# Four of sixteen row groups turned by DMA, and a deeper fold of the mirrored groups, in a fused FFT and state-space kernel

## The chip, the cores and the metric

The kernel runs on one core of a Trainium2 chip, in one launch. The metric is the device time of that launch in microseconds. A run of the kernel before has 306.61 us as its median of three (306.09 to 307.59).

## The reference

The input x has 2048 tokens of 1024 features, in bf16. Two results are mixed by a gate that is one number for each token:

```
g = sigmoid((x * gate_w).sum(-1))
a = irfft2(rfft2(x) * W)                       # over tokens and features
b = S5 recurrence: h_t = Lam_bar * h_(t-1) + B_bar x_t ;  b = 2 Re(C h) + x * Dskip
out = g * a + (1 - g) * b
```

The states h are 1024 complex numbers. Everything is kept in bf16 with float32 sums on TensorE.

## The kernel before, in words

The kernel is written as generators, one for each kind of step (turn a row group, fold it, multiply it, move a result out of PSUM, store it). The string ORDER holds one letter for each step, and the kernel is issued in the order of that string; PIECES gives the order in which the small vector steps of the recurrence (letter "v") are taken, and SLOTS says which of four PSUM buffers each product gets. No scheduler comes behind this: each engine works through its own part of the list in order, and semaphores make it wait for the others. So one instruction that waits holds up everything that its engine was given after it.

**The Fourier side.** The tokens are taken as 16 row groups j of 128 tokens. `load_x` reads x, two row groups to a DMA. `turn` (L901) turns a row group on TensorE with eight 128x128 transposes, and `turn_out` (L906) copies the result from PSUM into xQ on ScalarE. `fold` (L920 to L926) forms sums and differences of feature halves on VectorE: L920 the odd part, L922 the sums, L925 and L926 sums and differences of those. The first four row groups are folded one at a time, the others in pairs. For the pairs named in MIRROR (row groups 8 to 15) the odd part is folded once more: `mirror` (L942) reverses it on TensorE, and `fold_odd` (L948, L949) adds and subtracts. `fd` (L419 to L426) multiplies a row group by the tables in G_sb: the odd half with 4 matmuls of 512 columns (L423), or 4 of 256 where it is mirrored (L419), and the even half with 4 matmuls of 256 columns (L426). `fd_out` (L433) and `s1_out` (L458) move the results out of PSUM, some on VectorE (FD_DVE, S1_DVE) and the rest on ScalarE. `s1` (L446) is the next DFT stage; later come `s2`, `times_w` (L601), `is1` and `is2`, with turns through DRAM between them, and `spectral` (L809 to L828), which unfolds the inverse transform on VectorE.

**The recurrence side.** `unit_mm` (L387) multiplies xQ by the B tables, in 8 chunks c of 256 tokens; it needs all sixteen row groups in xQ and the B tables, which come as transposing DMAs (`load_B`, L248). `unit_out` (L397) copies to h on ScalarE. `recur` does the recurrence of one chunk on VectorE: products with tables (L336, L339), sums (L342, L345), the carry (L348), two scans (L352), the carry out (L357, L360), products again, and the two last operations L363 and L367, after which h of the chunk may be read. `early_mm`, `own_mm` (L697, L711) multiply h by C for one token tile of 128 at a time. Chunk 7 is token tiles 14 and 15, whose products are the last ones (L711); `last_out` (L883) scales and adds them on VectorE, and `last_store` writes them out. The last tile is cut at its end into two pieces of 256 columns:

```python
    rest[-1:] = [(15, K, H), (15, K + H, H)]
```

The angles of the tables are made on ScalarE for the indices in ANG_ACT (L268) and on VectorE for the rest (L270); the casts of the tables are on ScalarE for those in CAST_ACT and on GpSimd for the rest (L276, L283).

Of the kernel before, what the change touches and what calls it, by code (L numbers as in the profile page):

```python
# [21 lines left out]
D = 1024  # L22
# [7 lines left out]
NHA, NHB = 2, 1  # L30
NSEP = 2
DIAG = (10, 11, 12)

WARM = 7
FD_DVE = (0, 1, 3, 7, 8)
CAST_ACT = (6, 7)
ANG_ACT = (0, 4, 5, 6)
CARRY_POOL = ()
S1_DVE = (1, 2, 3)
CLOSES = (0, 1, 2, 3, 10, 4, 5, 11, 12, 6, 7, 8, 9)  # L40
PIECES = (
# [6 lines left out]
)  # L48
SLOTS = (
    "0123013201301230123012301230120312301320123023102310213021302130230123121320320123021321201323023120",  # L50
    "3201231031231203201230130121231023012301201201303201320132013231032103012031",
)
MIRROR = (6, 7, 8, 9)
ORDER = (
    "xTxUfTVVfxVGTVVUUfVaaTfGVffaFFfxTxff2UaEtfTfaxfFUTxk2SbUEffEUAxFx1TTSTfEUFTUtAFf2US1bTbEfffUbbbEASUA",
    "STfATU~FuTfUEtFUTfUFS~hbEtaEtFwuffFrtAttt1ttttStSb1bbgbbHErrf~AttffEfAFhb1uSttbErttSShetHtftrtfvttAv",
    "tbvktAAtvttHr1b1vvFverFheEtt~ttKHEhh1ttvSSttvtu11vccSHtvtHAtFhhtvKrwccc1tvvccAttAEHtHFEKKwvvtvhvvvvv",
    "vtc1cccttvc11SA1cvvvvwSvhhvvvvA1vKKsHecccHHenLssvvsssvvhMNMJWssnsnvHsssvNvWLMsvvvsvjvnsMJWYWMYMs3Mv4",
    "h4NJ53Nv54Hvvvvv45h6J7H7hvvjym35m44nv56n7H7YM56nv88v3NN78W8WJM8vvyn4+vvj754Nh5YvM+HmN+h34vvyvvh5vMMJ",
    "JWm8M6hH473m7Hh5+M+48ndmHHdvJY86v4+nv5n7NWMJ7N3J4yv8MYjn4vv56N7vvmN+vvX87h5v8v5vy3Jhv8m4+455H6mh7H78",  # L60
    "8nJYH6m77v+hNymn+HY+vvvyvnNNmh8+vvv8JqiivJqqvnimI+hihvvvviYqiJyYdIhNiivvqImiqHHInqiY+ImJHIiHyvvvIqmI",
    "vviIIII%+niiIvvvyINmN+hvvminidIvvnvIlvlhpXHlzXNplvvNJ+mzZHPzPzhhHlHZZZZZpYJJ+o+QmQRRyRJ+RRZDRzZplRZO",
    "ZRZDPzvZQoYQPBvvvvZDOolZvoOzlZOZRZZQDRoovzBlQRRvoBZZZZRZZRvBvQCDDDOOzDlpopvBBYDPYzZvZZDZQ9oZZQ0oPRDR",
    "9RyRRRCyD9oo9C909oY900QD000",
)

EVEN = ((0, 0), (2, 1), (2, 0), (0, 1))
# [6 lines left out]
def _host_consts():  # L74
# [7 lines left out]
        G[cls, :, 1] = -np.sin(ang)  # L82
    G[0, :, 1, 0] = (-1.0) ** np.arange(K)
    Ge = np.stack([G[0, :H, :, e::2] for e in range(2)])
    Go = np.stack([G[1, :, :, e::2] for e in range(2)], axis=1)

    n = np.arange(H)[None, :] + 0.5
    Gi = np.zeros((4, 2, P, H))
    for u in range(4):
# [35 lines left out]
    b16 = lambda z: np.ascontiguousarray(np.asarray(z, dtype=np.float32).astype(ml_dtypes.bfloat16))  # L125
    return dict(
        G=b16(np.concatenate([Go.reshape(4, P, 4 * K // 4).transpose(1, 0, 2).reshape(P, 4 * K),
                              Ge.reshape(2, 2, P, H).transpose(2, 0, 1, 3).reshape(P, 4 * H)], axis=1)),
        Gi=b16(Gi),
        T2=b16(np.concatenate([Ts, Tc, -Ts], axis=2)),  # L130
        K3=b16(np.stack([Kc, Ks], axis=1)),
# [7 lines left out]
def kernel(  # L139
# [58 lines left out]
    def psum(shape, name, dtype=FP32):  # L198
        return ps.tile(shape, dtype, name=name, tag=next(slots, "ps"), bufs=1 if SLOTS else 4)
# [20 lines left out]

    xn = [CT[i // 4][:, 2 * (i % 4):2 * (i % 4) + 2, :] for i in range(8)]
    x_v = x.rearrange("(p j) d -> p j d", j=16)
    fft = {}
    fft["G"] = pre.tile([P, 4 * K + 4 * H], BF16, name="G_sb")
# [184 lines left out]
    def fd():  # L409
        T2_sb, G_sb = fft["T2"], fft["G"]  # L410
        Go = G_sb[:, 0:4 * K].rearrange("p (d n) -> p d n", d=4)
        Ge = G_sb[:, 4 * K:4 * K + 4 * H].rearrange("p (e d n) -> p e d n", e=2, d=2)
        for j in range(16):
            psd = psf[j] = psum([P, 2, K], "ps_fd")
            if mirrored(j):
                odd = psd[:, 1, :].rearrange("p (e r m) -> p r e m", e=2, r=2)
                for r in range(2):
                    for d2 in range(2):
                        nc.tensor.matmul(odd[:, r], lhsT=preTs[j][:, 4 + 2 * r + d2, :], rhs=Go[:, d2].rearrange("p (e r m) -> p r e m", e=2, r=2)[:, r],  # L419
                                         start=(d2 == 0), stop=(d2 == 1))  # L420
# [3 lines left out]
            for e in range(2):  # L424
                for d2 in range(2):
                    nc.tensor.matmul(psd[:, 0, H * e:H * (e + 1)], lhsT=preTs[j][:, 2 * e + d2, :], rhs=Ge[:, e, d2, :],  # L426
                                     start=(d2 == 0), stop=(d2 == 1))
            yield

    def fd_out():  # L430
# [373 lines left out]
    def spectral(tbs):  # L804
        for tb in tbs[1::2]:
            part, eo = part_of(tb)
            ev = halves_of[:, 0:2, 0:K].rearrange("p i (c n) -> p i c n", c=2)
            xy = part[:, :, 0:K].rearrange("p i (s c n) -> p i s c n", s=2, c=2)
            nc.vector.tensor_add(out=ev[:, :, :, 0:P], in0=xy[:, :, 0], in1=xy[:, :, 1])  # L809
            yield  # L810
            nc.vector.tensor_sub(out=ev[:, :, :, H - 1:P - 1:-1], in0=xy[:, :, 0], in1=xy[:, :, 1])
# [12 lines left out]
            part = part.rearrange("p i (s c n) -> p i s c n", s=2, c=2)  # L824
            ga = part.rearrange("p i s c n -> p i s (c n)")
            nc.vector.tensor_add(out=ga[:, :, 0], in0=eo[:, :, 0], in1=eo[:, :, 1])
            yield
            nc.vector.tensor_sub(out=ga[:, :, 1], in0=eo[:, :, 0], in1=eo[:, :, 1])  # L828
            for t in (tb - 1, tb):
                gas[t] = ga[:, t % 2]  # L830
            yield

    def add_late():
# [61 lines left out]
    pts = {}  # L895

    def turn():
        for j in range(16):
            pt = pts[j] = psum([P, 8, P], "pt", BF16)
            for i in range(8):  # L900
                nc.tensor.transpose(out=pt[:, i, :], in_=xn[j // 2][:, j % 2, P * i:P * (i + 1)], identity=ident)  # L901
            yield

    def turn_out():
        for j in range(16):
            nc.scalar.copy(out=x_gjq[:, :, :, :, j, :].rearrange("p c d g q -> p d c g q"),  # L906
                           in_=pts.pop(j).rearrange("p d (c q g) -> p d c g q", c=NCH, g=2))
            yield

    def fold():  # L910
        for j, n in [(j, 1) for j in range(4)] + [(j, 2) for j in range(4, 16, 2)]:
# [10 lines left out]
            nc.vector.tensor_add(out=apart(pairs["s"][:, at]), in0=lo, in1=hi)  # L922
            yield
            s_lo, s_hi = pairs["s"][:, at, 0:2], pairs["s"][:, at, 2:4]
            nc.vector.tensor_add(out=pairs["t"][:, at, 0:2], in0=s_lo, in1=s_hi)  # L925
            nc.vector.tensor_sub(out=pairs["t"][:, at, 2:4], in0=s_lo, in1=s_hi)  # L926
            yield

    mirrors = {}
# [79 lines left out]
    def load_Wcols():  # L1009
        nc.gpsimd.memset(unit_w[:, 0:1], 1.0)  # L1010
        nc.gpsimd.memset(unit_w[:, 1:2], 0.0)
        nc.gpsimd.tensor_copy(out=Wp.rearrange("p r b c -> p (r b c)"), in_=xn[7][:, 0, 0:64])
        nc.gpsimd.tensor_copy(out=Wf, in_=xn[7][:, 0, 0:2])
# [166 lines left out]
```

## Time and profile before

| | before |
|---|---|
| median of 3 runs | 306.61 us |
| the profiled execution | 306.76 us, span 305.0 us |
| TensorE busy | 297.3 us (97%) |
| VectorE busy | 289.8 us (95%) |
| ScalarE busy | 186.6 us (61%) |
| GpSimd busy | 73.8 us (24%) |
| DMA engines, mean of the span | 194 GB/s |

The span is the time from the first to the last instruction in the profile; 1.76 us of the execution lie outside it. PE is TensorE, DVE is VectorE, ACT is ScalarE, POOL is GpSimd, SP is the engine that issues most DMAs. In a timeline the columns are start, duration, engine, line, operation, the tiles (out<-in), shapes and count; what stands in brackets is the idle time just before, and what ended it.

### The profile page before, as it was taken

To read this page: it belongs to the slowest core of one execution; us is meant where nothing else is said; L and a number is where in the kernel's file an instruction comes from. 1 tells how busy PE (TensorE), PEld (TensorE's weight loads), DVE (VectorE), ACT (ScalarE), POOL (GpSimd) and SP (SyncE) were. 2 spreads that over 40 slices of the span, in tenths; PEclk is the share of its full clock that TensorE was granted. 3 is DMA by queue.
4 is the path that set the end of the run, shared out by engine and by line. 5 is a ranking of instruction groups with operands and counts; after the bars stand their busy time and mean duration, and the time that the engine had idled before them with its cause. 6 is when DMAs were issued, how large, how long until landed. Compare 5 with 4: busy or idle time off the path is not lost.

```text
span 305.0 us, 6407 instructions
## 1 busy us (share of the span) xinstructions
PE 297.3 (97%) x2576; PEld 199.2 (65%) x2598; DVE 289.8 (95%) x335; ACT 186.6 (61%) x251; POOL 73.8 (24%) x100
## 2 busy tenths in 40 slices
PE   6999999999999999999999999999999999999995
PEld 3666768878864684377744766679775896555544
DVE  0999999999999999999999998999999999999995
ACT  3999998787721477556665975365875866342400
POOL 1110344467554002002110212011112134344130
PEclk9799999999999999999999999999999999999999
DMA  6989998499999997989959877885898368996975
GB/s 214 376 291 181 219 181 221 74 205 119 273 189 267 250 269 145 260 247 232 221 103 198 191 176 201 271 206 145 195 237 178 98 79 168 153 127 147 186 114 169
DMA packets 70141, 59.29 MB, mean 194 GB/s; under 512 B 40632, under 2 KB 57536, under 8 KB 70112
## 3 DMA queue, kind: packets, MB, share of 16 engines
q1 hardware_dynamic: 63120, 50.18, 63.4%
q0 software_dynamic: 6912, 8.69, 23.9%
q8 instruction: 20, 0.33, 0.5%
q14 instruction: 9, 0.07, 0.1%
q10 hardware_dynamic: 80, 0.01, 0.0%
HBM read 28.45 MB, written 23.08 MB: 169 GB/s over the span
## 4 chain that ended last, share of the span: by engine, by line
PE 91%; DVE 5%; DMA 2%; issue 1%; ACTq 0%; DVEq 0%
PE psu L387 37%; PE ps_y L697 29%; PE ps_q L711 7%; PE ps_is L613 3%; PE ps_is L645 2%; PE ps_id L794 2%; PE ps_s L446 2%; PE ps_fd L426 2%; DMA vec<-in_gate_w_dram 2%; PE ps_s L578 1%; PE ps_fd L419 1%; PE ps_id L790 1%; DVE X L433 1%; PE ps_fd L423 1%; DVE CT L458 1%
## 5 line engine op out<-in xcount | busy, mean ns | idle before, releaser
L387 PE MATMUL psu<-xQ,BT 128*128 128x256 bf16 x1024 | 116.3, 273 | 0.0
L387 PEld LDWEIGHTS <-BT 128*128 128x128 bf16 x1024 | 99.0, 98 | 16.9 <-issue 5.0
L697 PE MATMUL ps_y<-CT,h 128*128 128x512 bf16 x399 | 92.4, 379 | 0.8
L352 DVE TENSOR_TENSOR_SCAN h<-rz,h 128x2048 bf16<-128x2048 f32 (+1 forms) x20 | 71.1, 3577 | 0.0
L697 PEld LDWEIGHTS <-h 128*128 128x128 bf16 x416 | 39.8, 98 | 46.3 <-issue 2.5
L769 POOL DMA_DIRECT2D y_scratch<-su x20 | 17.5, 904 | 136.7 <-ACT su L763 91.0
L397 ACT CAST h<-psu 128x1024 bf16<-128x1024 f32 x32 | 32.3, 1012 | 17.3 <-PE psu L387 14.8
L339 DVE TENSOR_TENSOR h<-h,tab 128x4096 bf16<-128x4096 bf16 (+1 forms) x20 | 37.3, 1865 | 0.5
L728 ACT ACTIVATE ye<-ps_y,omg 128x512 f32<-128x512 f32 x26 | 17.5, 689 | 28.0 <-PE ps_y L703 13.4
L336 DVE TENSOR_TENSOR xQ<-h,tab 128x4096 bf16<-128x4096 bf16 x12 | 27.4, 2287 | 1.4 <-ACT h L397 1.2
L587 ACT CAST X<-ps_s 128x1024 bf16<-128x1024 f32 x16 | 16.1, 1008 | 15.0 <-PE ps_s L578 15.0
L655 ACT CAST ZT<-ps_is 128x1024 bf16<-128x1024 f32 x16 | 15.8, 1014 | 9.6 <-PE ps_is L645 9.6
L711 PE MATMUL ps_q<-CT,h 128*128 128x512 bf16 (+1 forms) x110 | 21.1, 348 | 0.1
L621 ACT CAST C<-ps_is 128x1024 bf16<-128x1024 f32 x16 | 16.1, 1014 | 8.0 <-PE ps_is L613 6.6
L835 POOL DMA_DIRECT2D BT<-y_scratch x10 | 14.4, 1592 | 22.0 <-DVE BT L828 12.1
L801 ACT ACTIVATE BT<-ps_id,gB 128x1024 bf16<-128x1024 f32 x14 | 15.3, 1115 | 6.6 <-PE ps_id L794 5.1
L711 PEld LDWEIGHTS <-h 128*128 128x128 bf16 x112 | 11.0, 98 | 9.4
L906 ACT COPY xQ<-pt 128x1024 bf16<-128x1024 bf16 x16 | 15.7, 1016 | 1.7 <-PE pt L901 1.7
L763 ACT ACTIVATE su<-xs,omg 128x512 f32<-128x512 bf16 x20 | 14.3, 723 | 0.7 <-DVE xs L753 0.6
L433 ACT CAST X<-ps_fd 128x1024 bf16<-128x1024 f32 x11 | 11.2, 1020 | 0.1
L920 DVE TENSOR_TENSOR preT<-xQ 128x1024 bf16<-128x1024 bf16 (+1 forms) x10 | 5.8, 579 | 5.2 <-ACT xQ L906 5.0
L901 PEld LDWEIGHTS <-CT 128*128 128x128 bf16 x128 | 8.7, 104 | 2.3 <-issue 1.5
(188 smaller groups left out, 395.3 us busy)
## 6 DMA issues: line engine op xcount, KB each, us to landing
y_scratch<-ye SPq DMA_DIRECT2D x20, 256.0 KB, 3.4
y_scratch<-su POOLq DMA_DIRECT2D x20, 256.0 KB, 4.5
Bb<-turn_scratch SPq DMA_DIRECT2D x16, 256.0 KB, 5.3
turn_scratch<-C SPq DMA_DIRECT2D x16, 256.0 KB, 3.8
raw<-turn_scratch SPq DMA_DIRECT2D x8, 512.0 KB, 3.7
CT<-in_A_x_dram SPq DMA_DIRECT2D x7, 512.0 KB, 7.4
xs<-in_A_x_dram SPq DMA_DIRECT2D x13, 256.0 KB, 3.0
out_dram<-BT SPq DMA_DIRECT2D x11, 256.0 KB, 3.6
```

Source lines behind the costliest of these rows:

```text
L336: nc.vector.tensor_mul(out=tmps["s"], in0=u[:, ::-1], in1=bc(i))
L339: nc.vector.tensor_mul(out=u, in0=u, in1=bc(i))
L352: nc.vector.tensor_tensor_scan(out=seg, data0=rz[:, js.start + j:js.start + j + m].rearrange("p j t -> p (j t)"), data1=seg, initial=0.0, ...
L387: nc.tensor.matmul(psu[:, j, :], lhsT=BT[4 * q + j][:, ri, d8, :], rhs=xQ[:, c, d8, :], start=(d8 == 0), stop=(d8 == 7))
L397: nc.scalar.copy(out=hs[c][:, ri, 4 * q:4 * q + 4].rearrange("p b (q j) -> p b q j", j=32), in_=psus.pop((c, q, ri)).rearrange("p b (j q) ...
L587: nc.scalar.copy(out=X2, in_=ps2s[g][b])
L621: nc.scalar.copy(out=C1.rearrange("p h (u i) -> p h u i", u=4), in_=pscs[g][t].rearrange("p h (i u) -> p h u i", u=4))
L655: nc.scalar.copy(out=ZT[:, 4 * kp:4 * kp + 4, :, 4 * G:4 * G + 4].rearrange("p (c r) n g -> p c r n g", c=2), in_=pszs.pop((G, kp)).rearra ...
L697: nc.tensor.matmul(psy, lhsT=hs[c][:, ri, jb, P * tq:P * (tq + 1)], rhs=CT[ri][:, jb, 512 * dh:512 * (dh + 1)], start=(i == 0), stop=(i == ...
L711: nc.tensor.matmul(psq, lhsT=hs[c][:, ri, jb, P * tq:P * (tq + 1)], rhs=CT[ri][:, jb, at:at + n], start=(i == 0), stop=(i == 15))
L728: nc.scalar.activation(out=ye, in_=psys[tb][:, K * hf:K * (hf + 1)], func=ACT.Copy, scale=omg[:, tb:tb + 1])
L769: nc.gpsimd.dma_start(out=y_dram[tb, hf], in_=xgs[tb, hf], accum_op=ALU.add)
```

## The change

- **Row groups 12 to 15 (NTURN = 12).** They are no longer loaded in two plain DMAs and turned on TensorE. Two transposing DMAs bring 64 rows of 4096 elements each straight into the place in SBUF where the plain rows lay, already turned, and `turn_out` copies them from there, with ScalarE as before, instead of from PSUM.
- **The even half of the mirrored row groups.** The lower quarter is folded once more on VectorE (one add in place, then an add and a subtract of half the size), and its product takes two matmuls of 128 columns where it took two of 256. A new table Gf of 256 columns comes with G_sb. The even product is now issued ahead of the odd one.
- **Tables.** The even table (with Gf) is loaded ahead of the odd one.
- **The last tile** is cut into 384 and 128 columns, not 256 and 256.
- **Who does what.** FD_DVE, S1_DVE, CAST_ACT and ANG_ACT name other indices: as many casts from PSUM on VectorE as before (5 and 3), one angle fewer there, and one table cast fewer on ScalarE and one more on GpSimd.
- **Order.** ORDER, PIECES and SLOTS are new throughout.

```diff
+NTURN = 12
-FD_DVE = (0, 1, 3, 7, 8)
-CAST_ACT = (6, 7)
-ANG_ACT = (0, 4, 5, 6)
+FD_DVE = (1, 2, 3, 5, 9)
+CAST_ACT = (5,)
+ANG_ACT = (2, 4, 5, 6, 7)
-S1_DVE = (1, 2, 3)
+S1_DVE = (1, 3, 4)
...
+    Gf = np.concatenate([G[0, :P, :, 2 * f::4].reshape(P, P) for f in range(2)], axis=1)
...
+    x_sg = x.rearrange("(s g j) d -> g s (j d)", g=2, j=16)
+    xt = CT[1][:, 4:8].rearrange("p a k -> p (a k)").rearrange("p (j d g s) -> p j d g s", j=4, d=8, g=2)
...
     def load_x():
         for i in range(8):
+            if i >= NTURN // 2:
+                g = i - NTURN // 2
+                nc.sync.dma_start_transpose(out=xt[:, :, :, g].rearrange("p j d s -> p (j d) s"), in_=x_sg[g][:, NTURN * D:])
+                yield
+                continue
...
-        for a, b in ((0, 4 * K), (4 * K, 4 * K + 4 * H)):
+        for a, b in ((4 * K, 4 * K + 5 * H), (0, 4 * K)):
...
         for j in range(16):
             psd = psf[j] = psum([P, 2, K], "ps_fd")
+            if mirrored(j):
+                even = psd[:, 0, 0:H].rearrange("p (r m f) -> p f r m", r=2, f=2)
+                for f in range(2):
+                    nc.tensor.matmul(even[:, f], lhsT=preTs[j][:, f, :], rhs=Gf[:, f], start=True, stop=True)
+            for e in range(1 if mirrored(j) else 0, 2):
+                for d2 in range(2):
+                    nc.tensor.matmul(psd[:, 0, H * e:H * (e + 1)], lhsT=preTs[j][:, 2 * e + d2, :], rhs=Ge[:, e, d2, :],
+                                     start=(d2 == 0), stop=(d2 == 1))
...
-    rest[-1:] = [(15, K, H), (15, K + H, H)]
+    rest[-1:] = [(15, K, K - P), (15, D - P, P)]
...
     def turn():
-        for j in range(16):
+        for j in range(NTURN):
...
     def turn_out():
         for j in range(16):
+            if j >= NTURN:
+                nc.scalar.copy(out=x_gjq[:, :, :, :, j, :].rearrange("p c d g q -> p d g c q"),
+                               in_=xt[:, j - NTURN].rearrange("p d g (c q) -> p d g c q", c=NCH))
+                yield
+                continue
...
             s_lo, s_hi = pairs["s"][:, at, 0:2], pairs["s"][:, at, 2:4]
-            nc.vector.tensor_add(out=pairs["t"][:, at, 0:2], in0=s_lo, in1=s_hi)
             nc.vector.tensor_sub(out=pairs["t"][:, at, 2:4], in0=s_lo, in1=s_hi)
+            if not mirrored(j):
+                nc.vector.tensor_add(out=pairs["t"][:, at, 0:2], in0=s_lo, in1=s_hi)
+            else:
+                nc.vector.tensor_add(out=s_lo, in0=s_lo, in1=s_hi)
+                nc.vector.tensor_add(out=pairs["t"][:, at, 0], in0=pairs["s"][:, at, 0], in1=pairs["s"][:, at, 1])
+                nc.vector.tensor_sub(out=pairs["t"][:, at, 1], in0=pairs["s"][:, at, 0], in1=pairs["s"][:, at, 1])
```

More of the change, by code (lines that the diff above doesn't have):

```diff
@@ L32 @@
 DIAG = (10, 11, 12)
+NTURN = 12
 WARM = 7
-FD_DVE = (0, 1, 3, 7, 8)
-CAST_ACT = (6, 7)
-ANG_ACT = (0, 4, 5, 6)
+FD_DVE = (1, 2, 3, 5, 9)
+CAST_ACT = (5,)
+ANG_ACT = (2, 4, 5, 6, 7)
 CARRY_POOL = ()
-S1_DVE = (1, 2, 3)
+S1_DVE = (1, 3, 4)
 CLOSES = (0, 1, 2, 3, 10, 4, 5, 11, 12, 6, 7, 8, 9)
 PIECES = (
[6 rows of a table removed]
[6 rows of a table added]
 )
 SLOTS = (
-    "0123013201301230123012301230120312301320123023102310213021302130230123121320320123021321201323023120",
-    "3201231031231203201230130121231023012301201201303201320132013231032103012031",
+    "0123013201302130120130210213023130123012301230213023012031203120132032122031320312310231232021303210",
+    "320301302130213203021302102310231021032132132130213021301302013213031203",
 )
@@ L54 @@
 ORDER = (
[L55 to L64, printed above, removed]
+    "xTxUTfVVVfxTVVUVfVraafGTfGFUxxtaUtffFfE2aatTxfTfFTUfTSEfFUrEUfTTfAkxx2fFUSTUUEffFAEUTfxfUS~FSbUfSAuE",
+    "FfFFEUSAUb1b1bE2bbbUAfabbbbbfAEtthtr~rgfwHtEfuSetASttftfA1b1btttF1FEttEtfhfHt~utvbb11ttvhSH1twtrvSFh",
+    "ttrrtttAE1tttKcccccthtth~vSSvhvAtttttttHwvtvHHfc1AvttAFStrtwu1KeFFHAEE1tvvhcEcc1SHtASShAtcvvtvveAvvt",
+    "tvvvvhc11cvvvvKKKK1cssHeevvscccvvHsshskMLnvvvHNMhvnvvsv3HvvsMNvssWJWnsssvvssvMn3hhjs44v55vMLvvNvvvJY",
+    "vMWMMWJYNH6v44v7H7hY53h5v44v86HvyjmmHv77M88JMn34h845567+vv5nvnnvNNhym++vW8Nv35vJvYvhmNH7JWjhJH68JMMW",
+    "yvWH44H7vvvm7nMYM38M5vvnnN548+6vvn+34vj5yv5vJXvvhdd7NJ7m84N5YMN45yv8vv6hm3++hn6Hm787Hm4vY8J+mHd4v5y+",
+    "N7Jh5Hm7Jvvn+Y86v8vv+nNm+7788JqqYhymNnhvvNiivqHhvviqiIIvmYqHiHIvId++hivvviyIvHvJqvvvvvvnimiyImIininJ",
+    "iqi+IINNmiqIIJIni+v%IiIIm+YJNvIJXvvhylH+zvvlhlNm+mzvZZvZZZZHzXYYpplhPPQvRRyRRJRhoQzZHpZRllZ+ZRDHZZvD",
+    "OovRvllPzzpoBQvlQZOPZvZZvDoBZZpQDzzDQORRBoooOBvRRZplDoZDOPOzRZZYZZRvvCvQBvozBZDZPZZZQoDDZRDR9oRQRQyR",
+    "o0R9oCy909CD09Y990D000Y",
 )
@@ L127, in _host_consts @@
         G=b16(np.concatenate([Go.reshape(4, P, 4 * K // 4).transpose(1, 0, 2).reshape(P, 4 * K),
-                              Ge.reshape(2, 2, P, H).transpose(2, 0, 1, 3).reshape(P, 4 * H)], axis=1)),
+                              Ge.reshape(2, 2, P, H).transpose(2, 0, 1, 3).reshape(P, 4 * H), Gf], axis=1)),
         Gi=b16(Gi),
@@ L222 @@
     x_v = x.rearrange("(p j) d -> p j d", j=16)
+    x_sg = x.rearrange("(s g j) d -> g s (j d)", g=2, j=16)
+    xt = CT[1][:, 4:8].rearrange("p a k -> p (a k)").rearrange("p (j d g s) -> p j d g s", j=4, d=8, g=2)
     fft = {}
-    fft["G"] = pre.tile([P, 4 * K + 4 * H], BF16, name="G_sb")
+    fft["G"] = pre.tile([P, 4 * K + 5 * H], BF16, name="G_sb")
     raw = t3p.tile([P, 6 * D], BF16, name="raw")
@@ L412, in fd @@
         Ge = G_sb[:, 4 * K:4 * K + 4 * H].rearrange("p (e d n) -> p e d n", e=2, d=2)
+        Gf = G_sb[:, 4 * K + 4 * H:].rearrange("p (f r m) -> p f r m", f=2, r=2)
         for j in range(16):
             psd = psf[j] = psum([P, 2, K], "ps_fd")
+            if mirrored(j):
[6 more added lines that the diff above has]
+                                     start=(d2 == 0), stop=(d2 == 1))
             if mirrored(j):
@@ L423, in fd @@
                     nc.tensor.matmul(psd[:, 1, :], lhsT=preTs[j][:, 4 + d4, :], rhs=Go[:, d4, :], start=(d4 == 0), stop=(d4 == 3))
[L424 to L427, printed above, removed]
             yield
@@ L825, in spectral @@
             ga = part.rearrange("p i s c n -> p i s (c n)")
+            for t in (tb - 1, tb):
+                gas[t] = ga[:, t % 2]
             nc.vector.tensor_add(out=ga[:, :, 0], in0=eo[:, :, 0], in1=eo[:, :, 1])
@@ L828, in spectral @@
             nc.vector.tensor_sub(out=ga[:, :, 1], in0=eo[:, :, 0], in1=eo[:, :, 1])
-            for t in (tb - 1, tb):
-                gas[t] = ga[:, t % 2]
             yield
@@ L1011, in load_Wcols @@
         nc.gpsimd.memset(unit_w[:, 1:2], 0.0)
-        nc.gpsimd.tensor_copy(out=Wp.rearrange("p r b c -> p (r b c)"), in_=xn[7][:, 0, 0:64])
-        nc.gpsimd.tensor_copy(out=Wf, in_=xn[7][:, 0, 0:2])
+        nc.gpsimd.tensor_copy(out=Wp.rearrange("p r b c -> p (r b c)"), in_=xn[5][:, 0, 0:64])
+        nc.gpsimd.tensor_copy(out=Wf, in_=xn[5][:, 0, 0:2])
         yield
```

12 rows, old and new, of the table PIECES are left out of this document.

## The prediction

> **What bounds the kernel now.** I read the page first: busy time, then the chain of work that ended last.
>
> ```profile
> span 305.0 us, 6407 instructions
> ...
> PE 297.3 (97%) x2576; PEld 199.2 (65%) x2598; DVE 289.8 (95%) x335; ACT 186.6 (61%) x251; POOL 73.8 (24%) x100
> ...
> PE 91%; DVE 5%; DMA 2%; issue 1%; ACTq 0%; DVEq 0%
> ```
>
> By the chain this is a TensorE kernel. But VectorE is nearly as full, so I looked in the timeline for the place where the two meet last, which is token tile 14, the first product that needs chunk 7.
>
> ```profile
> 286.20 1.22 DVE L367 TENSOR_TENSOR h<-h,xQ 128x2048 bf16<-128x2048 bf16 x1
> 301.57 0.48 DVE L883 SCALAR_TENSOR_TENSOR raw<-ps_q,omg,xQ 128x256 bf16<-128x256 f32 x1 [0.50 <-PE ps_q L711]
> 287.08 0.60 PE L794 MATMUL ps_id<-raw,ZT 128*128 128x256 bf16 x4
> 287.52 14.02 PE L711 MATMUL ps_q<-CT,h 128*128 128x512 bf16 x79
> ```
>
> VectorE ends the recurrence of chunk 7 at 286.20 + 1.22 = 287.42, and TensorE, just out of other work, begins tile 14 at 287.52. Behind that lie only the 14 us of tiles 14 and 15, one vector operation and the store. So both engines are the bound, within 0.1 us: the end moves by the smaller of two gains, that of TensorE up to 287.52 and that of VectorE up to 287.42. How much of VectorE's time is waiting, the list of waits tells:
>
> ```profile
> DVE xQ L336 <- ACT h L397: 1.2, 1, 1.2
> DVE raw L883 <- PE ps_q L711: 0.5, 1, 0.5
> DVE BT L809 <- ACT raw L801: 0.4, 1, 0.4
> DVE UV L601 <- PE ps_is L613: 0.2, 1, 0.2
> DVE preT L920 <- PE ps_fd L426: 0.2, 1, 0.2
> ```
>
> Once VectorE's start-up is over, it waits 2.0 us ahead of 287.42 (all but the 0.5 of L883), and each of these four waits is for a product of TensorE, direct or through ScalarE. All the rest is work.
>
> **TensorE's gain.** The chain of waits in order of time has the prices:
>
> ```profile
> 26.04 0.38 PE ps_r L942
> ...
> 29.46 0.45 PE pt L901 x8
> 29.91 0.44 PE ps_fd L419 x4
> ...
> 237.67 0.22 PE ps_id L790 x4
> ```
>
> Eight transposes are 0.45 us, so four row groups are 1.80. A matmul of 256 columns is 0.44 / 4 = 0.11, one of 128 columns 0.22 / 4 = 0.055; eight mirrored row groups each trade two of the first for two of the second, 8 x 2 x 0.055 = 0.88. Together 2.68. The new even product writes PSUM with a stride of two, which no row here shows; at half rate the 0.88 would be nothing, at full rate it is all there. I take it whole, since the pattern only changes where the results go. From 26.04 the chain is TensorE without a break, and there the whole of a saving counts; two of the four removed turns (0.90) lie behind that point, the other two just ahead of it, where TensorE still waits now and then. So the gain is 0.90 + 0.88 = 1.8 at least and 2.7 at most. I take 2.3, and 0.3 off for the B tables (below): 2.0.
>
> **VectorE's gain.** What it does ahead of 287.42, by kinds, in the two issue orders: eight operations of 128x256 more (the new fold, two for each of four pairs; the add in place replaces one of equal size), one angle fewer, and one L809 that now stands behind the last L367. Everything else is equal in count. An operation's price is the time from its start to the next one's:
>
> ```profile
> 10.72 0.29 DVE L925 TENSOR_TENSOR preT<-sums 128x256 bf16<-128x256 bf16 x1
> 10.93 0.28 DVE L926 TENSOR_TENSOR preT<-sums 128x256 bf16<-128x256 bf16 x1
> ```
> ```profile
> 19.13 0.34 DVE L270 TENSOR_SCALAR ang<-tau_f,ang 128x256 f32<-128x256 f32 x1
> 19.39 1.22 DVE L458 CAST CT<-ps_s 128x1024 bf16<-128x1024 f32 x1
> ```
> ```profile
> 290.86 0.42 DVE L809 TENSOR_TENSOR BT<-BT 128x512 bf16<-128x512 bf16 x1
> 291.20 0.42 DVE L811 TENSOR_TENSOR BT<-BT 128x512 bf16<-128x512 bf16 x1
> ```
>
> That is 8 x 0.21 = 1.68 more, 0.26 and 0.34 less: 1.08 us of work added, on an engine that has 2.0 us to give. This alone would eat the change. What speaks for it is the order. Operations that need the result of the one right before them cost more:
>
> ```profile
> 33.24 0.68 DVE L948 TENSOR_TENSOR preT<-preT,ps_r 128x512 bf16<-128x512 bf16 x1
> 33.95 0.69 DVE L949 TENSOR_TENSOR preT<-preT,ps_r 128x512 bf16<-128x512 bf16 x1
> 34.55 0.69 DVE L922 TENSOR_TENSOR sums<-xQ 128x1024 bf16<-128x1024 bf16 x1
> ```
>
> L949 waits for L948 and starts 0.03 after its end (33.24 + 0.68 = 33.92); L922 does not wait for L949 and starts 0.09 ahead of its end (34.64). A wait for the neighbour thus costs 0.12. Counting in the issue orders, from the first operation on the turned vectors to the last L367, the operations that wait for the one right before: 50 in the kernel before, 34 in the changed one, although 8 of these 34 are the new fold's. 16 x 0.12 = 1.9 less. So the work ahead of the meeting point is 1.08 - 1.9 = 0.8 shorter. Of the 2.0 of waits, the largest two (1.2 and 0.4) are for products that TensorE now makes about 2 us earlier; I count 1.6 as gone, and 0.4 for new waits that I can't see: 2.0 in all. The bounds are 0.8 (waits as now) and 2.8 (none left).
>
> The Trainium skill ("VectorE: DVE Perf Modes", section "The DRAIN you can't avoid") states a rule against the 1.9: a flush follows every vector operation, and eight copies took the same time with a semaphore after each as with one at the end. By that rule VectorE's part would be 1.08 longer ahead of waits. The rows above disagree, 0.03 after the end against 0.09 ahead of it, so I keep the 1.9 and give the rule a rival.
>
> **The turned x on the queues.** The two new DMAs stand on SP behind x of groups 10 and 11, ahead of the B tables. When do they land? In the kernel before, GpSimd's wait shows the landing of the last of x, and two rows of busy time by stretch (at their end the granted clock, the share of the DMA engines and GB/s) show the rates:
>
> ```profile
> 21.26 0.64 POOL L1012 COPY Wp<-CT 128x64 bf16<-128x64 bf16 x1 [12.38 <-DMA CT<-in_A_x_dram]
> ```
> ```profile
> 2.40:21.30 18.90, 17.03 (x142) 11.15 (x143) 13.77 (x38) 15.17 (x21) 0.88 (x5) 0.91 1.00 327
> 24.00:29.00 5.00, 4.89 (x47) 3.04 (x48) 4.93 (x9) 5.00 (x7) 0.00 (x0) 1.00 1.02 194
> ```
>
> And ScalarE's timeline shows when it would ask for them:
>
> ```profile
> 12.80 0.50 ACT L268 ACTIVATE ang<-tau_f,ang 128x256 f32<-128x256 f32 x1
> ...
> 23.02 1.03 ACT L433 CAST X<-ps_fd 128x1024 bf16<-128x1024 f32 x1
> 24.05 1.01 ACT L906 COPY xQ<-pt 128x1024 bf16<-128x1024 bf16 x1
> ```
>
> The last of x landed at 21.26, with the DMA engines full (share 1.00) at 327 GB/s on the way; the stretch from 24 to 29 holds transposing loads of B alone, also full, at 194 GB/s. Taken away are 1.05 MB of plain x (3.2 us at 327) and the one B table that stood ahead of it (0.26 MB, 1.3 at 194); added are 0.07 MB of Gf (0.2) and 1.05 MB turned (5.4): the turned x lands at about 21.26 - 4.5 + 5.6 = 22.4. ScalarE asks for it after 12 copies and 3 casts, where at 24.05 it had done 11 copies, 4 casts and one angle: 24.05 + 1.01 - 1.03 - 0.50 = 23.5. So the wait is covered by 1.1 us of ScalarE's own work, and I cost it at nothing. If the cover is gone, the copy holds up what is queued behind it on ScalarE: casts of `fd` and `s1` results, for whose PSUM buffers TensorE waits, and the last copies into xQ, without which `unit_mm` can't begin. The B tables as a whole land up to 5.4 - 3.2 = 2.2 later; TensorE has mirrored products and `s1` to do meanwhile, hence the 0.3 above (between 0 and 1).
>
> **Small things.** A copy out of SBUF instead of PSUM has the same size on the same engine; I count none. The even table comes first and 0.07 MB larger, so the odd one is 0.2 later, under even products that now run first: nothing. GpSimd gets one table cast more:
>
> ```profile
> L276 POOL CAST tab<-sn_f 128x512 bf16<-128x512 f32 x3 | 2.6, 883 | 16.0 <-ACT sn_f L1075 16.0
> ```
>
> This is 0.9 us on an engine that is busy a quarter of the time; if the chunk that needs the last table pair came first, VectorE would wait up to that much. The last cut shortens the end:
>
> ```profile
> 291.53 0.74 DVE L883 SCALAR_TENSOR_TENSOR raw<-ps_q,omg,xQ 128x512 bf16<-128x512 f32 x1
> ```
>
> From 512 to 256 columns L883 falls from 0.74 to 0.48, so 128 columns take about 0.35: 0.13 less.
>
> **The sum.** 306.76 (span 305.0 and 1.76 around it) less the smaller gain, 2.0 on either engine, less 0.13: 304.6. The profiled execution is 0.15 above the median of the runs, well inside their spread, so I leave it at that. About 0.5%, 1.5 us, is what a measurement of this kernel can tell from no change.
>
> **Rivals.** *The order saves no vector time.* Then VectorE is the bound, with 1.08 more work less 1.2 to 1.6 of waits: 306.76 - 0.3 - 0.13 = 306.3, no change. For it: both engines meet within 0.1 us. Against it: the three rows of L948, L949 and L922. Chance 0.13.
>
> *The turned x comes late,* the side on which it is slower. If 64 rows turn at half the rate of 128, the two DMAs take 10.8 and land at 27.8, 4.3 after ScalarE asks. TensorE loses that in its start-up, against 2.3 gained: 306.76 + 2.0 - 0.13 = 308.6. It decides from a landing about 2.3 after 23.5, that is 25.8, on. For it: no transposing load of 64 rows is in the trace, and 1.1 us is little cover. Against it: VectorE has folded work in hand there. Chance 0.20.
>
> *More comes free.* All four waits go and TensorE keeps its 2.7: 306.76 - 2.7 - 0.13 = 303.9, or lower if the start-up closes up too. Chance 0.10. The forecast keeps 0.57.
>
> **How the numbers follow.** The forecast's own bounds, 0.8 to 2.7, are 303.9 to 305.8; 0.46 of its 0.57 lies over 0.5% below 306.61, 0.11 within. The first rival gives 0.11 to no change and 0.02 to slower, the second 0.16 to slower and 0.04 to no change, the third 0.10 to faster: 0.56, 0.26, 0.18. The range reaches from 303.2, in the third rival, to 308.0, which leaves out the worse half of the second and the edge of the third.
>
> **What would show it.** In the changed profile: the last L367's counterpart ends near 285.4 and tile 14 starts then; VectorE's waits ahead of it sum to under 1 us; the first `unit_mm` starts no later than 31.48 less 1; ScalarE waits for no DMA before the first copy of the turned x. I am wrong if that copy waits over 2 us, if VectorE's end doesn't move (then the order's saving is not real), or if TensorE stands idle between the B tables' landing and 60 us.

## The result: slower by half a per cent

The changed kernel takes 308.30 us as the median of 22 runs, the kernel before, measured beside it, 307.02 us; the ratio is 1.0052 with a 95% interval of 1.0029 to 1.0074. The forecast was 304.6, and faster. The range up to 308.0 misses the time by 0.3.

The profiled execution took 307.81 us. Its page begins:

```profile
span 306.0 us, 6341 instructions
...
PE 295.3 (96%) x2542; PEld 196.0 (64%) x2566; DVE 289.7 (95%) x342; ACT 186.5 (61%) x251; POOL 77.6 (25%) x101
```

Against the page of before, TensorE is busy 2.0 us less and VectorE 0.1 less, though the span is 1.0 us longer. So the added time is idle time, not work. The timeline at the meeting place, tile 14, shows both engines late by the same amount:

```profile
287.51 1.22 DVE L376 TENSOR_TENSOR h<-h,xQ 128x2048 bf16<-128x2048 bf16 x1
285.10 17.50 PE L725 MATMUL ps_q<-CT,h 128*128 128x512 bf16 x94
```

VectorE ends chunk 7 at 287.51 + 1.22 = 288.73 (before 287.42). TensorE's row holds the last 16 products of tile 13 too, 16 x 0.216 = 3.5 us, so tile 14 begins at about 288.6 (before 287.52). The lists of waits, of VectorE and then of TensorE (us in total, times, longest), name what they stood for:

```profile
DVE UV L615 <- PE ps_is L627: 1.6, 1, 1.6
DVE BT L823 <- ACT BT L815: 1.3, 1, 1.3
DVE h L348 <- POOL tab L292: 1.2, 2, 0.7
DVE xQ L345 <- ACT h L406: 0.9, 1, 0.9
DVE Zp L555 <- PE zps L551: 0.3, 1, 0.3
```
```profile
PE aps L542 <- POOL Acol L487: 1.5, 1, 1.5
...
PE ps_fd L431 <- ACT SC L1099: 0.7, 1, 0.7
...
PE ps_s L460 <- ACT CT L472: 0.4, 1, 0.4
PE ps_fd L431 <- DVE X L447: 0.4, 1, 0.4
```

VectorE waits 5.3 us ahead of tile 14, where it waited 2.0: the 1.2 at 190 us is gone, and these five, between 47 and 244 us, have come or grown. TensorE's largest is new too, and it is for GpSimd, an engine that is busy a quarter of the time. GpSimd's timeline shows why:

```profile
66.38 1.14 POOL L1005 DMA_DIRECT2D z_scratch<-zsb  x1
67.52 0.62 POOL L292 CAST tab<-cs_f 128x512 bf16<-128x512 f32 x1
73.16 1.22 POOL L1008 DMA_DIRECT2D zt<-z_scratch  x1 [5.01 <-DMA z_scratch<-zsb]
74.37 6.64 POOL L487 COPY Acol<-A_last 128x2 bf16<-128x2 bf16 x4
```

The load of `zt` (a step of `gate_out`) reads back what the store of `z_scratch` wrote, so GpSimd stands 5.01 us until that has landed. The four last column copies (`keep_A1`) are queued behind it. They were so in the order of before too, but there the load had gone out at 51.63 us, long ahead of them; now it goes out at 73.16, and the first copy, whose source was ready at 66.7, starts at 74.37. TensorE needs the copies for `aps`, a step of `middle`; its row after, and the rows of copies and `aps` before:

```profile
81.06 0.23 PE L542 MATMUL aps<-ident,Acol 128*32 128x128 bf16 x1 [1.51 <-POOL Acol L487]
```
```profile
80.51 0.80 POOL L473 COPY Acol<-A_last 128x2 bf16<-128x2 bf16 x2
87.05 0.23 PE L528 MATMUL aps<-ident,Acol 128*32 128x128 bf16 x1
```

The copies end at the same time, 81.0 and 81.3. But the new order asks for them at 79.5 where the old one asked at 87.05: a margin of 5.7 us has become a wait of 1.5.

The wait for `z_scratch` is not all of it. For each of the two steps, the casts that make the sources and the copies, these rows give the shortest, the middle and the longest time in ns, and then the first and the last start:

```profile
L472 ACT CAST A_last<-ps_s x4: 999/1012/1018, 65.7 to 76.1; 128x1024 bf16<-128x1024 f32 x4
L487 POOL COPY Acol<-A_last x4: 393/1352/3728, 74.4 to 79.6; 128x2 bf16<-128x2 bf16 x4
```

The last source was ready at 77.15 us. If all four copies had taken 0.4 us, as the shortest did, they would have been done by 77.6 behind the same wait (an estimate). So two things make the 1.5 us: where the copies stand in GpSimd's queue, and how long they take there. The 22 runs lie in two groups, 16 at 307.05 to 308.69 and 6 at 310.25 to 311.38; the profile is of the first, so its rows explain that one alone, and what makes the second isn't known.

### The profile page after: what moved, and what is told of

It is laid out like the page before. It is cut to its first block, busy times and chain, and to the rows that moved or that the text cites. A ratio compares the mean times of both kernels' runs of the same rounds, so it can differ in the third digit from the quotient of the medians.

```text
span 306.0 us, 6341 instructions
## 1 busy us (share of the span) xinstructions
PE 295.3 (96%) x2542; PEld 196.0 (64%) x2566; DVE 289.7 (95%) x342; ACT 186.5 (61%) x251; POOL 77.6 (25%) x101
## 5 line engine op out<-in xcount | busy, mean ns | idle before, releaser
L711 PEld LDWEIGHTS <-h 128*128 128x128 bf16 x416 | 39.8, 98 | 46.5 <-issue 2.5
L783 POOL DMA_DIRECT2D y_scratch<-su x20 | 18.2, 925 | 136.8 <-ACT su L777 107.3
L725 PE MATMUL ps_q<-CT,h 128*128 128x512 bf16 (+2 forms) x110 | 21.0, 349 | 0.1
L849 POOL DMA_DIRECT2D BT<-y_scratch x10 | 12.8, 1490 | 23.4 <-DVE BT L844 16.0
L725 PEld LDWEIGHTS <-h 128*128 128x128 bf16 x112 | 10.2, 98 | 10.4 <-DVE h L376 0.3
L925 ACT COPY xQ<-pt 128x1024 bf16<-128x1024 bf16 x12 | 11.9, 1009 | 2.9 <-PE pt L915 2.9
L285 POOL CAST tab<-sn_f 128x512 bf16<-128x512 f32 x4 | 5.2, 1312 | 32.2 <-ACT sn_f L1099 32.2
L615 DVE TENSOR_TENSOR UV<-X,Wb 128x2048 bf16<-128x2048 bf16 x8 | 9.6, 1216 | 1.6 <-PE ps_is L627 1.6
```

Source lines behind the costliest of these rows:

```text
L711: nc.tensor.matmul(psy, lhsT=hs[c][:, ri, jb, P * tq:P * (tq + 1)], rhs=CT[ri][:, jb, 512 * dh:512 * (dh + 1)], start=(i == 0), stop=(i == ...
L725: nc.tensor.matmul(psq, lhsT=hs[c][:, ri, jb, P * tq:P * (tq + 1)], rhs=CT[ri][:, jb, at:at + n], start=(i == 0), stop=(i == 15))
L783: nc.gpsimd.dma_start(out=y_dram[tb, hf], in_=xgs[tb, hf], accum_op=ALU.add)
```

## Experiments

All ratios are to the kernel before, measured beside each run, with medians between 306.57 and 307.11.

### The parts in the old order

First theory: the parts are sound, and the new order brings the waits. Rivals: the turned x, or the fold, costs the time by itself. `old_turn` has the kernel before with `NTURN = 12` alone, `old_fold` the even fold with Gf alone, `old_all` everything but ORDER, PIECES, SLOTS and the lists of casts.

```diff
         for j in range(16):                                            # old_turn, in turn()
+            if j >= NTURN:
+                next(slots)
+                yield
+                continue
...
+                nc.vector.tensor_add(out=s_lo, in0=s_lo, in1=s_hi)     # old_fold, in fold()
...
+                    nc.tensor.matmul(even[:, f], lhsT=preTs[j][:, f, :], rhs=Gf[:, f], start=True, stop=True)
```

> Old order, with only row groups 12 to 15 turned by DMA (their eight-transpose steps on TensorE are gone, everything else stays). TensorE has 1.8 us less to do, VectorE nothing less. Theory 1 (the parts are sound, the new order brings the lost time, with waits of VectorE and TensorE for GpSimd): 306.0 to 307.0, no slower than the kernel before, since VectorE is the other bound and can only lose waits. Theory 2 (the two transposing DMAs cost the start-up: SP is held for 7 us, the B tables come later): 307.8 or more, with the first unit_mm over 0.5 us later than the 31.48 of before.

> Old order, with only the deeper even fold of the mirrored row groups (VectorE 8 operations of 128x256 more, 1.7 us; TensorE 0.9 us less). Theory 1 (parts sound): 306.5 to 307.5, VectorE's 1.7 us being partly taken out of its 2.0 us of waits. Theory 3 (the fold is what costs: VectorE is a bound and pays it in full): 308.0 to 308.5, VectorE's end of chunk 7 at 289.0 in place of 287.4.

> All parts of the change (turned x, even fold, tables, last cut) in the old order, with the old lists of who does which cast. Theory 1 (the order is at fault): 305.5 to 307.0, at least 1.3 us under the changed kernel's 308.3. Theories 2 and 3 (a part is at fault): 308.0 or more, the same as the changed kernel or worse.

`old_turn` 308.34, ratio 1.0054 (1.0035 to 1.0073); `old_fold` 310.98, 1.0143 (1.0125 to 1.0160); `old_all` 310.81, 1.0137 (1.0117 to 1.0156). In the old order both parts that were tried alone cost time, and the new order with its lists of casts wins back 2.5 of the 4.2 us that all parts cost. The first theory falls as far as the parts go.

Why `old_turn` is slower stays open. Its time is that of the second theory, but the sign of that theory is missing: the first `unit_mm` comes at 31.13 us, 0.35 earlier than in before and not over 0.5 later. With 1.8 us of turns less in the same order, TensorE idles 2.4 us from 7 to 31.3 us, where it idled 0.9, most of the difference in a wait for a result of `s1` that VectorE moves:

```profile
PE ps_r L959 <- DVE CT L466: 1.1, 1, 1.1
```

The profiled execution of `old_turn` took 307.08 us, 1.3 under the median of its runs, so the trace holds little of the time that was lost.

`old_fold` is slower than any theory had it. In it VectorE is busy 294.1 us against 289.8, and TensorE stands idle for 3.3 us between 31 and 60 us, where it never did before, most of it waiting for VectorE. The fold's operations come to 3.3 us more from start to start; the prediction's own prices, 8 x 0.21 and 8 waits for a neighbour at 0.12, give 2.6, or 0.66 for a pair. Three of the four pairs cost 0.62 to 0.65; the other cost 1.37, since two of its operations took 0.58 and 0.69 us where their like took 0.28 or 0.29. And TensorE gets nothing for it. Two mirrored row groups one after the other, in before and then in after:

```profile
49.22 0.60 PE L419 MATMUL ps_fd<-G_sb,preT 128*128 128x256 bf16 x4
49.65 0.60 PE L426 MATMUL ps_fd<-G_sb,preT 128*128 128x256 bf16 x4
50.09 0.60 PE L419 MATMUL ps_fd<-G_sb,preT 128*128 128x256 bf16 x4
```
```profile
65.59 0.39 PE L428 MATMUL ps_fd<-G_sb,preT 128*128 128x128 bf16 x2
65.78 0.42 PE L431 MATMUL ps_fd<-G_sb,preT 128*128 128x256 bf16 x2
66.03 0.60 PE L437 MATMUL ps_fd<-G_sb,preT 128*128 128x256 bf16 x4
66.47 0.38 PE L428 MATMUL ps_fd<-G_sb,preT 128*128 128x128 bf16 x2
```

From start to start a row group takes 50.09 - 49.22 = 0.87 before and 66.47 - 65.59 = 0.88 after. The two matmuls of 128 columns and the two behind them take 0.44 together (66.03 - 65.59), as the four of 256 columns did. Half the columns written with a stride of two cost as much as all of them written side by side. The loading of weights doesn't explain it: each transpose of 128 columns loads its own too, writes bf16 side by side, and takes 0.45 / 8 = 0.056 us in the prediction's rows. No run varied the stride itself.

### GpSimd's table casts

```diff
-CAST_ACT = (5,)
+CAST_ACT = (5, 6, 7)
```

> The changed kernel with table casts 6 and 7 back on ScalarE, as before (CAST_ACT 5, 6, 7), so that GpSimd has two casts less of 1.3 us each between 44 and 70 us. Theory 1 (GpSimd is overloaded there; VectorE waits 1.2 us for its tables, TensorE 1.5 us for its column copies): 306.3 to 307.3. Rival (these waits stand in for others that come right behind them, or ScalarE's casts delay products): 308.0 to 308.6, with other waits in the place of those for GpSimd.

307.88, ratio 1.0042 (1.0029 to 1.0055): hardly anything. TensorE's wait for `Acol` stayed 1.5, and VectorE's wait for its table at 69 us became 1.6 on ScalarE in place of 0.7 on GpSimd. Two casts less in GpSimd's queue don't help what stands behind the 5 us wait.

### One engine's work taken away

Second theory, after `old_fold`: VectorE alone paces the kernel. Each of these leaves out one piece of work, of TensorE (`old_less_pe`) or of VectorE.

```diff
-        for i in range(16):                                            # old_less_pe, in c_half
+        for i in range(8 if (tb, dh) == (0, 0) else 0, 16):
...
+            if c != 2:                                                 # old_less_dve, in out_re
                 nc.vector.tensor_add(out=u[:, 0], in0=u[:, 0], in1=tmps["s"][:, 0])
...
+            if n != 6:                                                 # old_less_start, in fold_odd
                 nc.vector.tensor_add(out=t[:, :, 6:8], in0=t[:, :, 4:6], in1=rev)
                 nc.vector.tensor_sub(out=t[:, :, 4:6], in0=t[:, :, 4:6], in1=rev)
```

> The kernel before, with 8 of the 16 matmuls of 512 columns of the first half of token tile 0 left out (half of that tile's product is missing): 8 x 0.216 = 1.7 us of TensorE work less, at about 84 us, nothing else changed. If TensorE is a bound of its own: 304.9. If both engines are bounds, met by chance, as the prediction says: 306.0 to 306.6 (VectorE's waits of 1.2 and 0.4 behind it go, VectorE's work stays). If VectorE alone paces the kernel and TensorE waits for it at every chunk: 306.3 to 306.9, VectorE's wait of 1.2 at 190 us unchanged.

> The kernel before, with the sum out_re of chunk 2 left out (one VectorE operation of 128x2048, 1.22 us; the real states of that chunk lack a term), nothing else changed. If both engines are bounds: 306.4 to 306.9, since TensorE's part stays. If VectorE alone paces the kernel: 305.2 to 305.6.

> The kernel before with the two fold_odd operations of the first mirrored pair left out (row groups 8 and 9 keep an unfolded odd part, so these rows of the spectrum are wrong): 2 x 0.69 us of VectorE work less at about 33 to 34 us, nothing else. If VectorE paces the start-up and everything behind it is passed on: 305.3 to 306.0. If a saving of VectorE is given back at the next place where it waits for TensorE (as with out_re of chunk 2, where 1.03 of 1.2 came back as a wait): 306.5 to 307.1, with a new wait of about 1 us.

Ratios 1.0000 (0.9980 to 1.0021), 0.9986 (0.9963 to 1.0009) and 0.9994 (0.9982 to 1.0006). None of the three cuts, of 1.7, 1.2 and 1.4 us, moves the time. In the trace of `old_less_dve`, VectorE's wait for h that was 1.2 in before is now two waits:

```profile
DVE xQ L336 <- ACT h L398: 2.3, 2, 1.3
```

It comes 1.24 us sooner to 134 us and waits 1.03 of that at 136.5 for TensorE's product. In `old_less_pe` TensorE, against its own start-up, is ahead by the whole cut at 86 us and has given it all back by 102, most of it in a wait of 1.2 for VectorE's `Bcol` at 91. So VectorE alone isn't the bound, and the second theory falls: the runs fit two engines that are tied, as the prediction had it, but at several places and not only at 287.5.

### Parts and waits in the new order

`new_nofold` is the changed kernel without the extra even fold, `new_zt_late` has the `zt` load behind the column copies, `new_turn_twice` puts TensorE work back into the start-up, `new_acol_act` gives the column copies to ScalarE.

```diff
-... cvvtvveAvvttvvvvhc11cvvvvKKKK1css ...       # new_zt_late, in ORDER: the third "e" (zt) goes behind the Ks
+... cvvtvvAvvttvvvvhc11cvvvvKKKKe1css ...
...
-            for i in range(8):                                         # new_turn_twice, in turn()
+            for i in tuple(range(8)) * (2 if j >= 8 else 1):
...
-            nc.gpsimd.tensor_copy(out=Acol[:, :, i], in_=A1s[i][:, :, 0])   # new_acol_act, in keep_A1
+            nc.scalar.copy(out=Acol[:, :, i], in_=A1s[i][:, :, 0])
```

> The changed kernel, its order and all its other parts kept, with the even half of the mirrored row groups as before (no extra fold, four even matmuls of 256 columns again): VectorE 8 operations and as many waits for a neighbour less, 8 x (0.21 + 0.12) = 2.6 us; TensorE 0.9 us more. If VectorE alone paces the kernel: 305.4 to 306.4, which would be under the kernel before. If both are bounds, or TensorE is: 308.0 to 309.2.

> The changed kernel with one letter of the order moved: the load of zt on GpSimd, which stands 5.0 us in front of the four column copies waiting for z_scratch to land, comes behind them. TensorE's wait of 1.5 us for Acol at 81 us should go. If TensorE's delay there is what VectorE pays later (0.87 at 92.9, 1.63 at 152, 1.30 at 244): 306.5 to 307.5. If those waits have causes of their own: 308.0 to 308.6, with the same waits in the same places.

> The changed kernel with the eight transposes of row groups 8 to 11 done twice (the second time into the same buffer, with the same result): 4 x 0.45 = 1.8 us of TensorE work put back into the start-up, as much as the turned x took away, nothing else. If TensorE is not what paces the start-up (VectorE and ScalarE feed it, and its saving only turned into idle time): 308.0 to 308.9, the first unit_mm within 0.4 of 31.28. If TensorE's start-up is on the path, as the prediction has it: 309.5 to 310.2.

> The changed kernel with the four last column copies (Acol of A_last) on ScalarE in place of GpSimd, so that they no longer stand behind the 5.0 us wait of the zt load, and the gate isn't put off either. TensorE's wait of 1.5 for Acol goes. If the new order loses its time there (TensorE a microsecond late from 81 us on, VectorE's waits of 0.87, 0.31 and 1.30 following): 306.8 to 307.5. If not: 308.0 to 308.6.

> Both: the changed kernel without the extra even fold and with the four column copies on ScalarE. Without the fold VectorE came 2 us earlier to 93 us and waited 2.07 there, with TensorE held 2.1 for Acol. If that hold is what ate the fold's cost: 305.8 to 306.8, under the kernel before. If the next hand-over (1.62 at 152 us) takes it all the same: 307.3 to 308.3.

| | median us | ratio to before |
|---|---|---|
| `new_nofold` | 308.25 | 1.0031 (1.0008 to 1.0055) |
| `new_zt_late` | 308.53 | 1.0045 (1.0026 to 1.0063) |
| `new_turn_twice` | 310.42 | 1.0128 (1.0100 to 1.0155) |
| `new_acol_act` | 306.10 | 0.9969 (0.9955 to 0.9984) |
| `new_nofold_acol_act` | 306.75 | 0.9998 (0.9980 to 1.0016) |

`new_acol_act` shows that the four copies on GpSimd are what makes the changed kernel slower than the kernel before. One line takes 2.2 us off its median (2.0 between the profiled executions, with spans of 306.0 and 304.0) and makes it faster than the kernel before, beyond the interval. That is more than the 306.8 to 307.5 that were expected. Its rows for the copies, for `aps` and for the last operation of chunk 7:

```profile
76.83 0.49 ACT L487 COPY Acol<-A_last 128x2 bf16<-128x2 bf16 x4
```
```profile
79.28 0.23 PE L542 MATMUL aps<-ident,Acol 128*32 128x128 bf16 x1
285.53 1.22 DVE L376 TENSOR_TENSOR h<-h,xQ 128x2048 bf16<-128x2048 bf16 x1
```

`aps` starts 1.78 us earlier than in the changed kernel (79.28 against 81.06; 0.2 of it is an earlier start-up), and every product behind it is 1.6 to 2.4 earlier. VectorE's waits of 0.9 and 0.3 just behind are gone and its chunk 7 ends at 286.75, not 288.73.

`new_zt_late` gained nothing: TensorE's wait for `Acol` fell to 0.4, but the gate came later and TensorE waited 2.0 for a buffer that ScalarE empties with a scale by that gate. The wait was moved, not removed. This run also parts the two causes that `new_acol_act` removes together. With nothing in front of them the last two copies still took 3.4 us on GpSimd, from 76.84 to 80.26, and ended too late. So taking the load out of their way mends 1.1 of the wait of 1.5; the rest hangs on the length of the copies.

`new_turn_twice` went the way of the prediction's reading, a little past its range: TensorE falls 1.7 behind by 23 us, is still 1.2 to 1.7 behind at the end, and its first `unit_mm` comes at 32.96, not 31.28. So turns put back into the start-up cost their 1.8 us there. That taking them away gains as much doesn't follow: in `old_turn` the first `unit_mm` came only 0.35 sooner. `new_nofold` shows nothing firm, since its 2.07 us wait for a product at 93.7 replaced the 0.9. With the copies mended too, the kernel without the fold is not faster than the one with it, though the fold brings TensorE nothing. In its profile VectorE stands idle for 0.5 to 0.6 us each at 36, 40 and 42 us, where the fold's operations were; the order was written for them.

### What bounds the mended kernel

The same cuts on top of `new_acol_act`, and two shifts of work between engines (`CAST_ACT = (5, 6, 7)`; `S1_DVE = (1, 2, 3, 4)`).

> The changed kernel with its four last column copies on ScalarE, and with 8 of the 16 matmuls of the first half of token tile 0 left out (half of that tile's product is missing): 1.7 us of TensorE work less. If TensorE alone sets the pace in the new order: 304.4 to 304.8. If VectorE is a bound too, as in the kernel before where the same cut gave nothing: 305.6 to 306.3.

> The changed kernel with its four last column copies on ScalarE, and with out_re of chunk 2 left out (1.22 us of VectorE work less; the real states of that chunk lack a term). If TensorE alone sets the pace: 305.9 to 306.4, with VectorE's next wait longer by 1.2. If VectorE is a bound too: 305.0 to 305.6.

> The changed kernel with its four last column copies on ScalarE, and table casts 6 and 7 on ScalarE too (GpSimd has two casts less). If TensorE alone sets the pace, VectorE's 1.2 us of waits for tables cost nothing: 305.9 to 306.5. If they count: 305.0 to 305.6.

> The changed kernel with its four last column copies on ScalarE, and the s1 result of row group 2 moved by VectorE in place of ScalarE. TensorE's wait of 0.40 at 26.4 us for it should go, and ScalarE's copies behind it come 1 us earlier; VectorE has 1.2 us more in its full start-up. If ScalarE is what holds TensorE in the start-up: 305.5 to 306.0. If VectorE's folds are: 306.3 to 307.2, with TensorE's waits for preT longer.

Ratios 0.9981 (0.9957 to 1.0005), 0.9965 (0.9947 to 0.9983), 1.0014 (0.9997 to 1.0031) and 1.0011 (0.9994 to 1.0028), against 0.9969 without them. Again neither cut helps alone. `acol_less_dve`, 306.01, is what TensorE alone as the bound would give, and in `new_acol_act` TensorE has no idle time from 31.3 to 288 us; but `acol_less_pe`, 306.82, is above both its readings. TensorE's timeline in that run shows where its 1.7 go:

```profile
93.77 0.62 PE L592 MATMUL ps_s<-Bb,KRS_sb 64*32 64x512 bf16 x15 [0.45 <-DMA Bb<-turn_scratch]
94.75 0.16 PE L523 MATMUL Zrev_ps<-Zp,JP_sb 128*128 128x2 bf16 x1 [0.36 <-DVE Zp L555]
```

It waits for a load, and then for VectorE. A wait that is added does count, though: with two casts more on ScalarE, VectorE's wait for a table at 70 us grows from 0.7 to 1.7, and the kernel is 1.3 to 1.7 us slower. My expectation had given that edit no way to lose. One result more on VectorE in the start-up (`acol_s1`) makes the first `unit_mm` 1.0 later, as the second reading had it.

Last, both cuts at once, with `if c != 0` in `out_re` for VectorE's part.

> The kernel before with 8 of the 16 matmuls of the first half of token tile 0 left out (1.7 us of TensorE work at 84 us; half of that product is missing) and out_re of both halves of chunk 0 left out (2 x 0.68 = 1.4 us of VectorE work ahead of 82 us; the real states of that chunk lack a term). If both engines are bounds that are tied to each other: about 1.2 less than the kernel before, 305.4 to 305.9. If something else (ScalarE, a DMA) is the bound: 306.5 to 307.1, as with either cut alone.

> The changed kernel with its four last column copies on ScalarE, and the same two cuts: half of the first product of token tile 0, and out_re of both halves of chunk 0. If both engines are bounds: 1.0 to 1.4 under the 306.1 without cuts, 304.7 to 305.1. If a DMA is the bound behind 93 us (the load of Bb, for which TensorE waited 0.45 with its own cut): 305.6 to 306.2.

`old_less_both` has a median of 305.97, 1.1 under before, as two tied engines would give; its ratio of 0.9978 has an interval of 0.9953 to 1.0003, so this is not shown beyond doubt. In its profile VectorE is 0.9 ahead from 81 us to the end, 0.3 of it from before the first cut. `acol_less_both` gained nothing: 306.10, 0.9977 (0.9960 to 0.9993). VectorE gave its cut back at once, at 69 us, to the table cast on GpSimd:

```profile
DVE h L348 <- POOL tab L292: 2.3, 2, 1.8
```

So in the new order the chain of table casts is a third bound at that place.

## Why the prediction was wrong

- **Both engines are bounds.** Right, as far as the runs show. They end within 0.2 us of each other at tile 14 again, and neither engine's cut alone moved the time; both cuts together gave 1.1 us in the old order, with an interval that just reaches no change. The argument took 287.5 as the one meeting place. The runs show others: at about 91 to 102 and at 136 us in the old order, and in the new one at 152 and 244 us, where VectorE waits for products of TensorE, direct or through ScalarE. In these runs a saving lasted only to the next one, while a delay went through all of them.
- **VectorE's work.** Right, and larger than forecast. From `vecF` to the end of chunk 7, less the listed waits, it was 279.7 - 2.0 = 277.7 and is 281.6 - 5.3 = 276.3: 1.4 shorter, forecast 0.8. The saving by order is real, although the sign that the prediction named for it, an earlier end of VectorE, did not come. By the rule of the Trainium skill ("VectorE: DVE Perf Modes", "The DRAIN you can't avoid") that was set against it, the work would have been 1.08 longer, and the trace goes against that; the same section adds that an operation that isn't held starts earlier, and with this the trace agrees (0.08 to 0.09 ahead of the end of the one before it).
- **VectorE's waits: a step that failed.** "I count 1.6 as gone, and 0.4 for new waits that I can't see"; 5.3 stand there. The order was read for what it does to VectorE and not for what it does to GpSimd, of which only the added cast was costed, at nothing, "on an engine that is busy a quarter of the time". A queue that stands still isn't busy. The load of `zt` had been moved from 51.6 to 73.2 us, right in front of the column copies, and TensorE's request for them from 87.05 to 79.5. Not all of the 5.3 hangs on that: with the copies on ScalarE 3.74 stay, of which 1.48 and 1.10 are waits for products at 150 and 242 us and 1.16 for table casts on GpSimd, a wait that the prediction named, priced at up to 0.9 and costed at nothing. No rival named the copies; the one that ended near the measured time, the turned x coming late, had another mechanism.
- **TensorE's gain: the term that was mis-sized.** The 0.88 of the even fold is 0.0, the lower end that was named (half rate) and not taken. Without it the prediction's sum is 0.9 to 1.8 for the turns less 0.3, so 0.6 to 1.5; with the copies mended tile 14 begins at 286.57, not 287.52, which is 0.95 sooner.
- **TensorE's start-up: also failed.** "From 26.04 the chain is TensorE without a break, and there the whole of a saving counts". `old_turn` is the plain test of it: the same order, the same granted clock in the start-up (0.93), 1.8 us of turns less, and the first `unit_mm` 0.35 sooner. For the new order, here is the busy time in two stretches, of before, of after and of `new_acol_act`:

```profile
7.00:31.30 24.30, 23.40 (x209) 15.18 (x212) 23.05 (x51) 22.66 (x29) 2.25 (x8) 0.93 1.02 276
...
60.00:100.00 40.00, 39.90 (x313) 28.49 (x314) 39.35 (x52) 20.49 (x28) 22.75 (x28) 1.00 1.10 210
```
```profile
7.00:31.30 24.30, 21.47 (x184) 13.15 (x188) 23.82 (x55) 22.08 (x27) 1.82 (x6) 1.00 1.07 271
...
60.00:100.00 40.00, 38.33 (x315) 27.22 (x315) 37.95 (x57) 21.90 (x29) 22.64 (x24) 1.00 1.08 213
```
```profile
7.00:31.30 24.30, 22.87 (x187) 13.72 (x188) 23.96 (x58) 22.20 (x28) 1.82 (x6) 0.93 1.07 271
...
60.00:100.00 40.00, 40.00 (x327) 27.96 (x322) 39.16 (x59) 22.32 (x35) 16.02 (x20) 1.00 1.09 215
```

The first figure behind the length is TensorE's. It idles 24.30 - 23.40 = 0.9 us in the start-up before and 2.8 after, 0.1 and 1.7 between 60 and 100. That is 3.5 us more waiting for 1.8 less work. The 1.1 by which it comes late to tile 14 is less than the difference, and part of the rest is the granted clock of the start-up, 0.93 before and 1.00 after. `new_acol_act`, whose start-up is issued in the same order, was granted 0.93: it was busy longer and idled 1.4 there, not 2.8, and its first `unit_mm` was no later, 31.08. So a faster TensorE bought nothing in that stretch. In after, the first `unit_mm` came at 31.28, not 30.5, with one product of `fd` more done by then.
- **The turned x.** Right as to its cover, but in the old order it was no gain: `old_turn` is 0.5% slower than before, and why is open. In the changed kernel ScalarE takes it first at 24.60 (forecast 23.5) and waits for no DMA:

```profile
24.60 1.05 ACT L921 COPY xQ<-CT 128x1024 bf16<-128x1024 bf16 x1
```

Of the 3.7 us between forecast and result, `new_acol_act` gives back 2.2. The other 1.5 fit the 0.9 that the fold was to bring and the start-up's waits; that split is argued, not shown.

## What to carry to other kernels

When an issue order is new, follow every queue through it, the idle engine's first: an instruction there that waits for a DMA to land holds up all that is queued behind it, a copy of two columns can take over a microsecond there, and what counts is the margin between the end of the last of these and the moment when a bound engine asks for it. Where two engines were tied, as here, a delay on either was paid and a saving on one alone bought nothing, so a change should be costed by what it does to both between each two meeting places. A small product is cheaper only if its output pattern lets it be: give an unknown rate both its ends in the sum, not only in the range.

## What the runs showed of the hardware

- TensorE writing float32 sums to PSUM with a stride of two took as long for 128 columns as for 256 side by side: 0.44 us for such a pair and the two matmuls behind it, the same as for four of 256.
- The smallest copies are not small on GpSimd: four of 128x2 took 6.64 us there (74.37 to 81.0) and 0.49 us on ScalarE. The longest took 3.73 us, from 74.70 to 78.43, and ended with a scan of VectorE that ran from 76.16 to 78.44; whether the one held up the other was not tested. In `new_zt_late` four such copies took 0.20, 0.75, 2.15 and 1.34 us.
- The first of the two transposing DMAs for x held SP for 7.08 us while it was issued, the second for 3.21, against 1.31 for a B table (in `old_turn` the two took 7.12 together):

```profile
8.40 7.08 SPq L236 DMA_TRANSPOSE CT<-in_A_x_dram  x1
...
16.15 3.21 SPq L236 DMA_TRANSPOSE CT<-in_A_x_dram  x1
19.40 1.31 SPq L257 DMA_TRANSPOSE BT<-in_B_B_re_dram  x1
```
